# An attention and gated-convolution kernel: batch 0's q and k loaded six tokens per partition, the gates' second half copied out by ScalarE, and a searched order of work

## The chip, the cores and the metric

The kernel runs on 1 core of one Trainium2 chip. The metric is the device time of one execution in microseconds (us), lower is better. A plain run of the kernel before is timed three times; one more execution is taken with the hardware profiler.

## The reference, cut to what matters

Two stages, fused by the kernel: attention with a local window of 96 tokens, 8 global tokens and a linear distance bias, then a projection, a convolution over the whole sequence by FFT, two gates and an output projection.

```python
# q, k, v: (4 batches, 8 heads, 768 tokens, 64);  n_global = 8, n_local = 96
scores = q @ k.transpose(0, 1, 3, 2) / sqrt(64)
rel = pos[:, None] - pos[None, :]
keep = (pos[None, :] < 8) | ((rel >= 0) & (rel < 96))
dist = where(is_global & ~is_local, 96, abs(rel))
a = softmax(where(keep, scores - slopes[h] * dist, -1e9))
x = (a @ v) as (4, 768, 512)
x1, x2, x3 = split(x @ w_proj)              # w_proj: 512 x 1536
conv = irfft(rfft(x2, axis=1) * rfft(filter, axis=0))
out = (x1 * conv * x3) @ w_out              # float32
```

## The kernel before, in words

**Data.** Everything between the loads and the output is float16, sums in PSUM are float32. PSUM is eight banks, held as four tiles of two (`bank0` to `bank3`). A key tile is 120 keys behind the 8 global keys; seven of them cover the 768 tokens, in three groups of two, two and three tiles (`GRP`). A head pair (`hp`, 0 to 3) fills the 128 partitions with two heads of 64.

**Attention of a batch** (`attention`): q and k are transposed on TensorE (`transposes`), the copies out of PSUM fill `QT` and `KT`; `scores` gives one group of a head pair; ScalarE takes the exponential into `E` (864 columns); VectorE multiplies by a mask of decays (`E<-E,mask`), except in batch 0, where TensorE adds the distances first (`near` times `slope`), so that batch 0 needs no mask. `values` multiplies with v, which carries a column of ones; `rc` and `xn` normalise; `transpose_x` and its copy give `xT`. Then `gate` makes, for a quarter of the channels (`j`) and half the tokens (`s`), x1 and x3 in two banks: x1 goes to SBUF (`x`), and VectorE multiplies x3, read from PSUM, by x1 into `g` (line 881). There are 32 such gates in the program, 8 per batch. `butterfly` folds `xT` into what the convolution needs.

**Convolution of a batch** (`conv`): `proj`, its copies `ab`, `fwd` (discrete Fourier matrices), the copies `X`, the products with the filter's spectrum (`p1`, `p2`, `sums`), `inv`, the copies `eo`, the mixing (`mix`), `half` and `y*g` (line 1014), six `out` projections per batch, their copies `ot` and the stores.

**Loads.** A transfer that changes float32 to float16 is issued by GpSimd (POOL), which is how k, v, the weights and the filter come, and q of the later batches. Batch 0's q comes in float32 over the SP queue: six tiles of 128 tokens by 8 heads, 1024 pieces of 256 bytes each, into the six output buffers `ot`, and ScalarE or VectorE casts each into `qn` (`load_q`, line 402 for the issue). Batch 0's k tiles (960 pieces of 256 bytes) alternate with its v tiles on POOL, ahead of the weights.

**What sets the order.** The program is a graph of operations (`Plan.op`), each with a modelled cost on every engine that may run it. `schedule` is a list scheduler: it takes the operation that can start first, with ties inside a small slack broken by a rank (its batch's due time, its place in it, and a bias), and picks the engine that ends it first, by the modelled costs plus `FAVOUR` on VectorE. Banks are chosen in the same pass. The engines then run their lists strictly in that order. Where TensorE's list leaves a gap, `fill` puts in multiplications of a dummy tile (`idle`, line 382), so TensorE stays at work. The times in the planner are its own and set only the order.

Of the kernel before, what the change touches and what calls it, by code (L numbers as in the profile page):

```python
# [59 lines left out]
class Op:  # L60
    __slots__ = ("cost", "fn", "preds", "succs", "wait", "tail", "bias", "acq", "use", "n",
                 "start", "end", "ready", "eng", "bytes", "batch", "table", "name", "order", "first", "landed")


class Plan:
# [55 lines left out]
    def schedule(self):  # L121
        for o in self.ops:
            for x in o.preds:
                x.succs.append(o)
            o.ready = 0.0
# [6 lines left out]
        for o in self.ops:  # L132
            o.first = set()
            for b in o.acq:
                for u in b.users:
                    o.first |= self.outer(u, {o}, o)
            o.first -= o.preds | {o}
            o.wait = len(o.preds) + len(o.first)
        after = {}
        for o in self.ops:  # L140
            for x in o.first:
                after.setdefault(x, []).append(o)
        total = {}
        for o in self.ops:
            o.tail = total.get(o.batch, 0.0)
            total[o.batch] = o.tail + o.cost.get("P", 0.0)
        free = {e: BEGIN for e in "PAVGS"}
# [5 lines left out]
        key = lambda o: o.batch[0] + o.batch[1] * o.tail / (total[o.batch] or 1.0) + o.bias  # L153
        while live:
            best = None
            for o in live:
                at = o.ready
                where = None
                if o.acq:
# [8 lines left out]
                    if at == math.inf:  # L168
                        continue
                e, s = min(((e, max(at, free[e])) for e in o.cost),  # L170
                           key=lambda x: (x[1] + o.cost[x[0]] + self.FAVOUR * (x[0] == "V"), x[0]))
                got = (s, key(o), o, e, where)
# [38 lines left out]
        return self.program(self.fill(out))  # L211

    BUSY = 0.225
    FAVOUR = 0.0
# [78 lines left out]
class Fused:  # L293
    PERIOD = 40.0
    NEAR = 3
    LATER = ()
    WL = [], [], [], [(0, 256), (1024, 256), (256, 256), (1280, 256), (512, 512)]
# [25 lines left out]
    def buffers(self):  # L323
# [34 lines left out]
        self.ot = [t(f"ot{i}", [P, DM], F32) for i in range(6)]  # L358
# [59 lines left out]
    def load_q(self, b, t):  # L418
        src = self.q[b, :, P * t:P * t + P, :].rearrange("h p d -> p h d")
        if b == 0:  # L420
            st = self.ot[t].rearrange("p (h d) -> p h d", h=self.H)
            self.load("S", st, src, [("ot", t)], (1024, 256), f"q{t}")
            self.g.op("AV", {"A": act(512), "V": dve(512, 2)}, lambda e: self.copy(
                e, self.qn[:, t], st), r=[("ot", t)], w=[("qn", t)], name="cast")
        else:
            self.load("G", self.qn[:, t], src, [("qn", t)], (1024, 256), f"q{t}")
# [23 lines left out]
    def setup(self):  # L450
# [21 lines left out]
        for lo, hi in ((0, 2), (2, 7)):  # L472
            g.op("V", dve(512 * (hi - lo), 4), lambda _, lo=lo, hi=hi: v.memset(self.kn[0:NG, lo:hi], 0.0),
                 w=[("kz", t) for t in range(lo, hi)], bias=-4500 if lo == 0 else -3500)
# [73 lines left out]
    def distances(self):  # L548
# [33 lines left out]
        for half in range(2):  # L582
            for k in range(2):
# [5 lines left out]
                g.op("AV", {"A": act(216) + act(264), "V": dve(216, 4) + dve(264, 4)}, spread,  # L589
# [5 lines left out]
        for half in range(2):  # L595
            ps = slice(64 * half, 64 * half + 64)
            for hp in range(4):
                dst = self.slope[ps, hp].rearrange("p k c -> p (k c)")
                dst = dst[:, 0:256].rearrange("p (k c) -> p k c", k=2)
                for k in range(2):  # L600
                    g.op("AV", {"A": act(64), "V": dve(64, 2)}, lambda e, ps=ps, hp=hp, k=k: self.times(
# [4 lines left out]
    def masks(self):  # L606
        g, nc, NL, n = self.g, self.nc, self.NL, 216
        v, dg, far, mask = nc.vector, self.dg, self.far, self.mask
        for hp in range(4):
# [13 lines left out]
            g.op("V", 2 * dve(400, 4) + 2 * dve(216, 4), spread, r=["far"] + [  # L623
# [105 lines left out]
    def scores(self, hp, gi, near=False):  # L729
# [27 lines left out]
        more = ([("near", i, k) for i in range(2) for k in range(2)] + [  # L757
# [17 lines left out]
    def values(self, j, c, slot):  # L775
# [43 lines left out]
        g.op("V", 0.09 + 0.05 * nt, lambda _: nc.vector.reciprocal(rc, view()[:, :, :, D:D + 1]),  # L819
             use=bs, w=[key], name="rc")  # L820
        g.op("AV", {"A": 4 * nt * act(D), "V": dve(4 * nt * D, 1, True)}, scaled, use=bs, r=[key],
# [41 lines left out]
    def gate(self, b, j, s):  # L863
# [4 lines left out]
        for o in (0, 2 * self.DM):  # L868
# [12 lines left out]
        g.op("V", dve(h, 1, True), lambda _: nc.vector.tensor_mul(  # L881
            gt[:, j, h * s:h * s + h], pts[1].f32()[:, 0:h], x1), use=[pts[1]], r=[key],
            w=[("g", b % 2, j, s)], name="g")

    def attention(self, b):
        self.g.batch = (self.PERIOD * (b - 1 + self.SHIFT), self.PERIOD * self.LONG)
        for c in range(3):
            new = ([0, 1, 2], [3, 4], [5])[c]
            for t in new:
                self.transposes("q", t, self.qn[:, t], P * t)  # L890
            for t in self.GRP[c]:
                self.transposes("k", t, self.kn[:, t], P * t)
            for i in range(4):
                self.scores(i, c, c < self.NEAR if b == 0 else (i, c) in self.LATER)
# [87 lines left out]
    def mixed(self, js):  # L982
# [4 lines left out]
        def run(_):  # L987
            v.tensor_sub(t, z, u)
            v.tensor_scalar(u, u, 2.0, None, op0=Alu.mult)
            v.tensor_add(z, z, u)  # L990
            v.tensor_sub(u, t, w)
            v.tensor_add(w, t, w)
        self.g.op("V", 4 * dve(512 * n, 2) + dve(512 * n, 4), run, name="mix", w=[
            ("mixed", jp) for jp in js] + [
            ("eo", jp, jj, par) for jp in js for jj in range(2) for par in range(2)])

    def gated(self, b, jps, half):
# [14 lines left out]
        g.op("V", dve(512 * n, 2) + dve(256 * n, 2), join, r=[("mixed", jp) for jp in jps] + [  # L1012
# [47 lines left out]
    def load_first(self):  # L1060
# [3 lines left out]
        for c in range(3):  # L1064
            for t in ([0, 1, 2], [3, 4], [5])[c]:
                self.load_q(0, t)
            if c == 1:
                self.first_rows(vt)
            runs = [(t, 1) for t in self.GRP[c]]
            for t, n in runs:  # L1070
                self.load_run(("kn",), self.kn, self.k, t, n)
            if c == 0:
                self.distances()
# [110 lines left out]
```

## Time and profile before

| | |
|---|---|
| median of 3 runs | 190.96 us (190.31 to 191.09) |
| the profiled execution's own time | 190.2 us |
| its span | 188.4 us |
| TensorE (PE) busy | 174.0 us, of it 11.4 us dummy multiplications |
| VectorE (DVE) busy | 166.1 us |
| ScalarE (ACT) busy | 144.0 us |
| GpSimd (POOL) busy, mostly issuing transfers | 76.6 us |
| TensorE clock granted | 1.0 throughout |

The span runs from the first to the last record; the run's own time is 1.8 us longer. A line such as `L881 DVE ... x32 | 17.1, 549 | 3.9 <-PE ...` says: line 881, 32 instructions, together 17.1 us busy (overlap taken out), 549 ns mean of one, 3.9 us of idle time on the engine just before them and who ended it. In a timeline, the first number is the start and the second the time until the last of the merged instructions ended. In the table by windows, each engine has its busy time and its count of instructions. The waits of one engine do not add to the span unless the chain that ends last runs through them.

### The profile page before, as it was taken

To read this page: it belongs to the slowest core of one execution; us is meant where nothing else is said; L and a number is where in the kernel's file an instruction comes from. 1 tells how busy PE (TensorE), PEld (TensorE's weight loads), DVE (VectorE), ACT (ScalarE), POOL (GpSimd) and SP (SyncE) were. 2 spreads that over 40 slices of the span, in tenths; PEclk is the share of its full clock that TensorE was granted. 3 is DMA by queue.
4 is the path that set the end of the run, shared out by engine and by line. 5 is a ranking of instruction groups with operands and counts; after the bars stand their busy time and mean duration, and the time that the engine had idled before them with its cause. 6 is when DMAs were issued, how large, how long until landed. Compare 5 with 4: busy or idle time off the path is not lost.

```text
span 188.4 us, 4561 instructions
## 1 busy us (share of the span) xinstructions
PE 174.0 (92%) x1742; PEld 105.7 (56%) x1742; DVE 166.1 (88%) x378; ACT 144.0 (76%) x292; POOL 76.6 (41%) x97
## 2 busy tenths in 40 slices
PE   7877999999899999899898999999998999999891
PEld 2345886656445667575355567754466675447440
DVE  6898875998999969999997869999999999999960
ACT  7389983568999999988967669859869576588352
POOL 8799993599989999993000000000000000000000
PEclk9999999999999999999999999999999999999999
DMA  6999999999999999999053000000260000005244
GB/s 134 197 167 149 153 196 209 154 153 152 143 171 145 154 141 140 142 151 132 4 220 117 0 3 0 3 0 2 80 257 1 5 0 0 3 29 194 111 165 169
DMA packets 90916, 20.47 MB, mean 109 GB/s; under 512 B 83816, under 2 KB 87824, under 8 KB 90896
## 3 DMA queue, kind: packets, MB, share of 16 engines
q0 software_dynamic: 80912, 12.14, 95.6%
q1 hardware_dynamic: 9984, 8.06, 13.6%
q8 instruction: 13, 0.21, 0.5%
q14 instruction: 7, 0.06, 0.1%
HBM read 25.84 MB, written 6.29 MB: 171 GB/s over the span
## 4 chain that ended last, share of the span: by engine, by line
DVE 42%; PE 32%; ACT 13%; issue 4%; SPq 4%; DMA 3%; DVEq 0%; ACTq 0%
PE bank L873 13%; PE bank L970 5%; DVE E L772 4%; SPq L402 4%; DVE g L881 4%; ACT E L765 4%; DMA ot<-in_q_dram 3%; DVE xn L814 3%; DVE y L1014 3%; PE bank L922 2%; PE bank L944 2%; DVE pp L1039 2%; ACT xn L818 2%; ACT QT L386 2%; PE bank L790 2%
## 5 line engine op out<-in xcount | busy, mean ns | idle before, releaser
L873 PE MATMUL bank<-xT,w 128*128 128x384 f16 x256 | 45.0, 326 | 0.2 <-ACT xT L386 0.2
L765 ACT ACTIVATE E<-bank 128x864 f16<-128x864 f32 x48 | 40.1, 910 | 1.2 <-PE bank L751 0.6
L873 PEld LDWEIGHTS <-w 128*128 128x128 f16 x256 | 24.3, 98 | 16.3 <-issue 1.3
L402 POOL DMA_DIRECT2D kn<-in_k_dram x28 | 26.6, 960 | 0.7 <-issue 0.5
L402 POOL DMA_DIRECT2D vn<-in_v_dram x28 | 25.6, 928 | 2.5 <-DMA w<-in_moe_w_proj_dram 1.9
L390 ACT ACTIVATE x<-bank 128x384 f16<-128x384 f32 x29 | 14.7, 508 | 12.7 <-PE bank L873 10.5
L970 PE MATMUL bank<-wo,y 128*128 128x512 f16 x96 | 21.9, 379 | 1.1 <-DVE y L1014 1.0
L772 DVE TENSOR_TENSOR E<-E,mask 128x864 f16<-128x864 f16 x36 | 20.5, 594 | 1.2 <-ACT E L765 1.1
L881 DVE TENSOR_TENSOR g<-bank,x 128x384 f16<-128x384 f32 x32 | 17.1, 549 | 3.9 <-PE bank L873 3.6
L390 ACT ACTIVATE ot<-bank 128x512 f32<-128x512 f32 x21 | 12.5, 597 | 8.2 <-PE bank L970 8.1
L402 POOL DMA_DIRECT2D qn<-in_q_dram x18 | 16.2, 910 | 5.0 <-DMA g<-in_moe_filter_fft_dram 3.5
L751 PE MATMUL bank<-QT,KT 64*128 64x216 f16 (+2 forms) x224 | 15.8, 241 | 2.0 <-ACT E L765 0.9
L970 PEld LDWEIGHTS <-y 128*128 128x128 f16 x96 | 9.0, 98 | 13.1 <-DVE y L1014 3.1
L790 PE MATMUL bank<-vn,E 128*128 128x65 f16 x224 | 15.5, 193 | 0.9 <-ACT E L765 0.8
L814 DVE TENSOR_TENSOR xn<-bank,rc 128x512 f16<-128x512 f32 (+1 forms) x21 | 16.1, 771 | 0.2
L390 ACT ACTIVATE ab<-bank 128x512 f16<-128x512 f32 x21 | 12.5, 611 | 4.0 <-PE bank L922 3.9
L790 PEld LDWEIGHTS <-E 128*128 128x128 f16 x224 | 14.0, 97 | 2.6 <-DVE E L772 0.7
L795 PE MATMUL bank<-vn,E 128*128 128x65 f16 x192 | 15.2, 193 | 0.0
L386 ACT CAST eo<-bank 128x384 f16<-128x384 f32 x29 | 12.9, 509 | 1.7 <-PE bank L947 1.2
L751 PEld LDWEIGHTS <-KT 64*128 64x128 f16 x224 | 8.5, 94 | 9.2 <-issue 5.8
L386 ACT CAST X<-bank 128x512 f16<-128x512 f32 x21 | 11.9, 606 | 2.2 <-PE bank L700 2.1
L795 PEld LDWEIGHTS <-E 128*128 128x128 f16 x192 | 13.2, 97 | 0.6 <-issue 0.3
(141 smaller groups left out, 361.6 us busy)
## 6 DMA issues: line engine op xcount, KB each, us to landing
out_dram<-ot SPq DMA_DIRECT2D x24, 256.0 KB, 2.6
kn<-in_k_dram POOLq DMA_DIRECT2D x28, 120.0 KB, 6.0
vn<-in_v_dram POOLq DMA_DIRECT2D x28, 120.0 KB, 6.7
qn<-in_q_dram POOLq DMA_DIRECT2D x18, 128.0 KB, 6.7
ot<-in_q_dram SPq DMA_DIRECT2D x6, 256.0 KB, 5.8
w<-in_moe_w_proj_dram POOLq DMA_DIRECT2D x4, 256.0 KB, 6.6
g<-in_moe_filter_fft_dram POOLq DMA_DIRECT2D x1, 768.0 KB, 11.9
w<-in_moe_w_proj_dram POOLq DMA_DIRECT2D x1, 512.0 KB, 8.6
```

Of the source, the lines that this page charges most:

```text
L386: {"A": nc.scalar.copy, "V": nc.vector.tensor_copy, "G": nc.gpsimd.tensor_copy}[e](out, in_)
L390: self.nc.scalar.mul(out, in_, c)
L402: return self.g.op(eng, 0.57 + 0.00035 * nbytes[0] if eng == "G" else 0.5, lambda _: e.dma_start(dst, src), w=w, r=r, nbytes=nbytes, name= ...
L751: nc.tensor.matmul(bs[hh].f32()[:, off:off + w], self.KT[hs, hp, P * m:P * m + P], self.QT[hs, hp, KL * m:KL * m + w], start=(off == 0 and ...
L765: g.op("A", act(864), lambda _: nc.scalar.activation(eo, bs[0].two()[:, :, 0:432].rearrange("p h (m w) -> p h m w", m=2), Act.Exp, scale=s ...
L772: g.op("V", dve(864, 2), lambda _: nc.vector.tensor_mul(eo, eo, mk), r=[("E", hp, gi), ("mask", hp)], w=[("E", hp, gi)], name="masked")
L790: nc.tensor.matmul(o[:, n, hh], ef[:, at:at + P], vt[:, t, 2 * hp + hh, :], start=first, stop=(t == 0), skip_group_check=True)
L795: nc.tensor.matmul(o[:, n, hh], ef[:, at:at + P], vt[:, t - 1, 2 * hp + hh, :], start=False, stop=True, skip_group_check=True)
L814: nc.vector.tensor_mul(to, o[:, :, :, 0:D], rc.to_broadcast([P, 2, 2 * nt, D]))
L873: nc.tensor.matmul(bk.f32()[:, 0:h], self.w[:, c, o + P * j:o + P * j + P], self.xT[:, c, h * s:h * s + h], start=(c == 0), stop=(c == 3))
L881: g.op("V", dve(h, 1, True), lambda _: nc.vector.tensor_mul(gt[:, j, h * s:h * s + h], pts[1].f32()[:, 0:h], x1), use=[pts[1]], r=[key], w ...
L970: nc.tensor.matmul(bk.f32(), y[:, c, P * t:P * t + P], self.wo[:, c, :], start=(c == 0), stop=(c == 3))
```

## The change

Four things change.

1. **q and k of batch 0** come by head pair: `load_pair` loads two heads with six consecutive tokens in each partition, so 256 pieces of 1536 bytes, all eight transfers on the SP queue (q into the `ot` buffers, k into `h1` and `h2`). The cast writes them as `[token of six][head]`. `transpose_pair` transposes six times 128 columns into one bank, and the copy out of PSUM puts the tokens back in order: it reads with a step of 128 columns where the old copy read neighbours. k is unpacked in two copies, and the global columns are spread per head pair. `attention(0)` now takes all three score groups of a head pair before the next pair. POOL keeps only v, weights and filter for batch 0.
2. **The gates** (`TWICE` holds all 32): ScalarE copies x3 out of PSUM as float16, and VectorE multiplies two float16 tiles in SBUF.
3. **The planner's numbers**: modelled costs of some operations (`near`, `spread`, `rc`, `xn` on ScalarE, `vfirst`), `FAVOUR` 0.1 instead of 0, `mixed` as five operations instead of one, the slopes on ScalarE only.
4. **The order**: before laying the list, `schedule` adds to ranks and engine preferences what a list of 40 seeds draws (`shake`), found by a search.

The diff, cut to its core:

```diff
+    def schedule(self):
+        self.prepare()
+        for seed in self.SEEDS:
+            self.shake(seed)
+        return self.program(self.fill(self.lay()))
+
+    def shake(self, seed):
+        r = random.Random(seed)
+        if r.random() < 0.4:
+            groups = sorted({(o.name, o.batch) for o in self.ops if o.eng not in "GS"})
+            g, by = r.choice(groups), r.gauss(0.0, 5.0)
+            lean = r.gauss(0.0, 0.3)
...
-        key = lambda o: o.batch[0] + o.batch[1] * o.tail / (total[o.batch] or 1.0) + o.bias
+            o.rank = o.batch[0] + o.batch[1] * o.tail / (total[o.batch] or 1.0) + o.bias + o.noise
...
-    FAVOUR = 0.0
+    SEEDS = (5, 6, 10, 30, 55, 82, 86, 89, 90, 94, 176, 184, 198, 209, 262, 321, 423, 503, 556,
...
+    FAVOUR = 0.1
...
+    TWICE = frozenset((b, j, s) for b in range(4) for j in range(4) for s in range(2))
...
+    def load_pair(self, what, hp):
+        hs, n = slice(2 * hp, 2 * hp + 2), what + "n"
+        if what == "q":
+            st, keys = self.oq[:, 768 * hp:768 * hp + 768], [("ot", i) for i in range(6)]
+        else:
+            st = (self.h1, self.h2)[hp // 2].bitcast(F32).rearrange("p a b -> p (a b)")
+            st, keys = st[:, 768 * (hp % 2):768 * (hp % 2) + 768], []
+        self.load("S", st.rearrange("p (h x) -> p h x", h=2),
+                  (self.q if what == "q" else self.k)[0, hs].rearrange("h (p r) d -> p h (r d)", r=6),
+                  [("stage", what, hp)], (256, 1536), what)
+        to = (self.qn if what == "q" else self.kn)[:, 0:6, hs].rearrange("p r h d -> p h r d")
+        self.g.op("AV", {"A": act(768), "V": 0.9}, lambda e: self.copy(
+            e, to, st.rearrange("p (h r d) -> p h r d", h=2, r=6)), r=[("stage", what, hp)] + keys,
+            w=[(n, "pair", hp)], name="cast")
+
+    def transpose_pair(self, what, hp):
...
+            for r in range(6):
+                nc.tensor.transpose(b.f16()[:, P * r:P * r + P], src[:, r, 2 * hp:2 * hp + 2, :],
+                                    self.ident)
...
+            g.op("AV", {"A": act(768), "V": dve(768, 1, True)}, lambda e: self.copy(
+                e, self.QT[:, hp].rearrange("p (n r) -> p n r", r=6),
+                b.f16()[:, 0:768].rearrange("p (r n) -> p n r", r=6)), use=[b],
+                w=[("QTp", hp)], name="qT")
...
-        g.op("V", dve(h, 1, True), lambda _: nc.vector.tensor_mul(
-            gt[:, j, h * s:h * s + h], pts[1].f32()[:, 0:h], x1), use=[pts[1]], r=[key],
-            w=[("g", b % 2, j, s)], name="g")
+        x3, ko = gt[:, j, h * s:h * s + h], ("g", b % 2, j, s)
+        if (b, j, s) in self.TWICE:
+            g.op("A", act(h), lambda _: nc.scalar.copy(x3, pts[1].f32()[:, 0:h]), use=[pts[1]],
+                 w=[ko], name="x3")
+            g.op("V", dve(h, 2), lambda _: nc.vector.tensor_mul(x3, x3, x1), r=[key], w=[ko], name="g")
+            return
...
     def attention(self, b):
         self.g.batch = (self.PERIOD * (b - 1 + self.SHIFT), self.PERIOD * self.LONG)
+        if b == 0:
+            for hp in range(4):
+                self.transpose_pair("q", hp)
+                self.transpose_pair("k", hp)
+                for c in range(3):
+                    self.scores(hp, c, True, True)
...
-        for c in range(3):
-            for t in ([0, 1, 2], [3, 4], [5])[c]:
-                self.load_q(0, t)
-            if c == 1:
+        for hp in range(4):
+            self.load_pair("q", hp)
+            self.load_pair("k", hp)
+            if hp == 0:
+                self.distances()
+            if hp == 1:
                 self.first_rows(vt)
...
+        for t in range(7):
+            self.load_run(("vn", 0), vt, self.v, t, 1)
```

**Where instructions move.** First, GpSimd's list at the start of the program, before (`dg` and `far` are the tables of distances from which the score biases are made):

```order
masks.py:199 AFFINE_SELECT ident<-ident 128x128
L402 DMA kn<-in_k_dram 120x8x64 x2
L557 IOTA dg 128x216
L562 AFFINE_SELECT dg<-dg 128x216 x2
L557 IOTA dg 128x48
...
L402 DMA vn_63<-in_v_dram 120x8x64 x2
L577 AFFINE_SELECT far<-far 8x120 x2
L402 DMA kn<-in_k_dram 120x8x64 x2
L402 DMA vn_63<-in_v_dram 120x8x64 x2
L402 DMA kn<-in_k_dram 120x8x64 x3
L402 DMA vn_63<-in_v_dram 120x8x64 x3
L402 DMA w<-in_moe_w_proj_dram 128x4x256 x3
```

and the same place now:

```order
masks.py:199 AFFINE_SELECT ident<-ident 128x128
L631 IOTA dg 128x216
L636 AFFINE_SELECT dg<-dg 128x216 x2
...
L440 DMA vn_63<-in_v_dram 120x8x64
L651 AFFINE_SELECT far<-far 8x120 x2
L440 DMA vn_63<-in_v_dram 120x8x64 x6
L440 DMA w<-in_moe_w_proj_dram 128x4x256 x4
```

Seven k transfers left this queue, two of which stood ahead of the tables of distances, and the weights follow v at once.

Second, ScalarE's list from the first bias table to the fourth exponential, before (buffer `bank_121` to `bank_124` are the PSUM tiles, `E_67` to `E_70` the four head pairs' exponentials, `mask` the decays for the later batches):

```order
L386 COPY near<-dg 64x264
L612 ACTIVATE mask<-dg 128x216
...
L386 CAST qn<-ot_103 128x512
L386 COPY QT<-bank_122 128x4x128
L386 CAST qn<-ot_104 128x512
L765 ACTIVATE E_67<-bank_123 128x2x2x216
L765 ACTIVATE E_68<-bank_124 128x2x2x216
L765 ACTIVATE E_69<-bank_121 128x2x2x216
```

and now (`h_85` and `h_86` hold k of pairs 0, 1 and 2, 3 in float32):

```order
L424 COPY near<-dg 64x264
L424 CAST qn<-ot 128x2x6x64
L686 ACTIVATE mask<-dg 128x216
L424 CAST kn<-h_85 128x2x6x64
L424 COPY KT<-bank_116 128x6x120
L424 COPY KT<-bank_116 128x120
L424 CAST qn<-ot 128x2x6x64
L424 CAST kn<-h_86 128x2x6x64
...
L840 ACTIVATE E_67<-bank_118 128x2x2x216
L840 ACTIVATE E_67<-bank_119 128x2x2x216
L424 CAST kn<-h_86 128x2x6x64
L840 ACTIVATE E_67<-bank_116 128x2x2x216
```

The exponentials go by head pair, and the cast of the last pair's k stands between the second and the third of them.

Third, VectorE's list where the first gates are multiplied, before (`x_95` to `x_98` are the four x1 buffers, `g_87` the gates of batch 0):

```order
L814 TENSOR_TENSOR xn_72<-bank_124,rc_106 128x2x384
L881 TENSOR_TENSOR g_87<-bank_123,x_95 128x384
L881 TENSOR_TENSOR g_87<-bank_121,x_96 128x384
L881 TENSOR_TENSOR g_87<-bank_122,x_97 128x384
L881 TENSOR_TENSOR g_87<-bank_124,x_98 128x384
L386 COPY xT<-bank_124 128x2x288
```

and now:

```order
L571 TENSOR_SCALAR y<-y 128x512
L960 TENSOR_TENSOR g_87<-g_87,x_95 128x384
L931 TENSOR_TENSOR xo<-xab,xcf 128x2x256
L960 TENSOR_TENSOR g_87<-g_87,x_96 128x384
L933 TENSOR_SCALAR xcf<-xcf 128x2x256
```

The gates no longer read a bank, and they alternate with the folds of the butterfly, where before four of them stood in a row.

138 lines of the change are left out of this document (83 added, 55 removed).

## The prediction

> **What bounds the kernel now.** I read the page first: busy times, slices, and the chain that ended last by engine.
>
> ```profile
> span 188.4 us, 4561 instructions
> PE 174.0 (92%) x1742; PEld 105.7 (56%) x1742; DVE 166.1 (88%) x378; ACT 144.0 (76%) x292; POOL 76.6 (41%) x97
> DVE  6898875998999969999997869999999999999960
> ACT  7389983568999999988967669859869576588352
> DVE 42%; PE 32%; ACT 13%; issue 4%; SPq 4%; DMA 3%; DVEq 0%; ACTq 0%
> ```
>
> No engine rules alone: VectorE holds most of the chain and is full from the middle on, TensorE is nearly as full, ScalarE is full only from slice 10 to 17. So I cut the span at three places of the program: the first gate (27.0 us), the product `y*g` of batch 0 (93.8, both kernels stand there at the same TensorE work, dummies left out), and the last `y*g` (182.2). The products end here, in VectorE's timeline:
>
> ```profile
> 91.95 1.82 DVE L1014 TENSOR_TENSOR y<-y,g 128x1536 f16<-128x1536 f16 x2
> ...
> 181.65 0.56 DVE L1014 TENSOR_TENSOR y<-y,g 128x768 f16<-128x768 f16 x1
> ```
>
> From the table by windows, first all work, then that of line 382 (the dummies) alone:
>
> ```profile
> 0.00:27.00 27.00, 22.83 (x325) 15.20 (x326) 22.20 (x78) 20.96 (x53) 25.05 (x40) 1.00 1.68 164
> 27.00:93.80 66.80, 63.65 (x636) 38.68 (x633) 60.66 (x131) 57.23 (x111) 51.56 (x58) 1.00 2.16 144
> 93.80:182.20 88.40, 85.20 (x778) 50.88 (x776) 83.22 (x170) 64.00 (x128) 0.00 (x0) 1.00 0.15 58
> 42.00:84.00 42.00, 39.49 (x434) 24.71 (x433) 38.96 (x87) 40.27 (x81) 39.57 (x45) 1.00 2.46 149
> 24.00:42.00 18.00, 18.00 (x221) 12.30 (x216) 14.35 (x36) 10.79 (x19) 12.48 (x15) 1.00 1.84 179
> ...
> 27.00:93.80 66.80, 2.06 (x8) 0.66 (x8) 1.00 2.16 144
> 93.80:182.20 88.40, 1.41 (x5) 0.49 (x5) 1.00 0.15 58
> ```
>
> The columns are PE, PEld, DVE, ACT, POOL. In the last stretch VectorE works 83.2 of 88.4 us and ScalarE 64.0: there VectorE sets the pace. In 42 to 84 ScalarE works 40.3 of 42 and VectorE 39.0: both are full. TensorE can give back its idle time and its dummies: 66.8 - 63.65 + 2.06 = 5.2 us in the middle, 88.4 - 85.2 + 1.41 = 4.6 after it.
>
> **The change part by part.** The groups of instructions with shapes, of which I use busy time over count:
>
> ```profile
> L881 DVE TENSOR_TENSOR g<-bank,x 128x384 f16<-128x384 f32 x32 | 17.1, 549 | 3.9 <-PE bank L873 3.6 <-ACT x L390 0.2
> L1046 DVE TENSOR_TENSOR X<-pp 128x512 f16<-128x512 f16 x8 | 3.3, 414 | 0.0
> L1010 DVE TENSOR_TENSOR y<-eo 128x256 f16<-128x256 f16 x4 | 1.1, 282 | 0.0
> L386 ACT CAST eo<-bank 128x384 f16<-128x384 f32 x29 | 12.9, 509 | 1.7 <-PE bank L947 1.2
> L818 ACT ACTIVATE xn<-bank,rc 128x64 f16<-128x64 f32 x28 | 6.0, 371 | 1.1 <-DVE rc L819 1.1
> L814 DVE TENSOR_TENSOR xn<-bank,rc 128x512 f16<-128x512 f32 x14 | 9.5, 682 | 0.1
> L814 DVE TENSOR_TENSOR xn<-bank,rc 128x768 f16<-128x768 f32 x7 | 6.6, 949 | 0.1
> L386 DVE COPY xT<-bank 128x480 f16<-128x480 f16 x11 | 4.3, 394 | 2.7 <-PE bank L835 2.7
> L386 ACT COPY xT<-bank 128x480 f16<-128x480 f16 x5 | 2.9, 588 | 0.5 <-PE bank L835 0.5
> L386 DVE COPY QT<-bank 128x512 f16<-128x512 f16 x5 | 2.1, 412 | 0.1
> L392 DVE TENSOR_SCALAR ot<-bank 128x512 f32<-128x512 f32 x3 | 2.0, 669 | 0.0
> L390 ACT ACTIVATE ot<-bank 128x512 f32<-128x512 f32 x21 | 12.5, 597 | 8.2 <-PE bank L970 8.1
> ```
>
> *Gates.* The product costs VectorE 17.1/32 = 0.53 us. From SBUF in float16 it lies between the 256- and 512-column products of two float16 tiles, 0.28 and 0.41: 0.345, so 0.19 less, 32 times 6.1 us. ScalarE gains a copy of 384 columns out of PSUM, like `eo`: 12.9/29 = 0.445, 32 times 14.2.
>
> *Moves between engines*, counted in the two orders: all 28 `xn` pieces leave ScalarE (-6.0) for three on VectorE (2 x 0.68 + 0.95 = +2.3); six `xT` copies go the other way (-2.3, +3.5); two `ot`, an `ab` and an `x` too (-2.6, +2.3). With the start's changes, VectorE comes out about 7 us lighter and ScalarE 17 heavier: the two together do more work than before, and what counts is where each of them was waited for. `mixed` as five operations issues the same five instructions, so it costs nothing by itself; other operations of VectorE may now stand between them, which only the order decides.
>
> *The start*, for which I read ScalarE's timeline, TensorE's, and the chain:
>
> ```profile
> 2.59 1.82 ACT L390 ACTIVATE slope<-ident 64x64 bf16<-64x64 f16 x11 [0.36 <-DVE slope L594]
> 7.85 1.39 ACT L386 COPY near<-dg 64x216 bf16<-64x216 bf16 x4 [3.43 <-DVE dg L571]
> 9.26 1.32 ACT L612 ACTIVATE mask<-dg 128x216 f16<-128x216 bf16 x6
> 12.19 0.62 ACT L386 CAST qn<-ot 128x512 f16<-128x512 f32 x1
> 24.44 3.24 ACT L765 ACTIVATE E<-bank 128x864 f16<-128x864 f32 x4
> ...
> 12.42 0.54 PE L742 MATMUL bank<-near,slope 64*128 64x432 bf16 x4
> 27.02 5.36 PE L873 MATMUL bank<-xT,w 128*128 128x384 f16 x32
> 32.22 0.50 PE L835 MATMUL bank<-ident,xn 128*128 128x128 f16 x6
> ...
> 33.98 0.26 PE L521 MATMUL bank<-cst,one 1*128 1x256 f16 x1
> ...
> 8.27 5.85 DMA ot<-in_q_dram
> 100.05 3.40 ACT xn L818 x16
> ```
>
> ScalarE's 3.4 us wait for `dg` goes, since two k transfers leave POOL ahead of the tables. Its new list up to the twelfth exponential: 16 slopes at 0.165 = 2.65, six `near` at 0.35 = 2.1, five casts at 0.8 (0.62 for 512 columns, and 0.69 ns for each more, as between `eo` and `ot`) = 4.0, two unpackings of k at about 1.05 (a cast's time and a small piece) = 2.1, ten masks at 0.2 = 2.0, twelve exponentials at 3.24/4 = 0.81 = 9.7: 22.6 us from 2.4, so 25.0 without a wait, against 27.7 (24.44 + 3.24). With a microsecond of waits for first scores, and then values, `xn`, `trx` and `xT` of the last pair (0.5 + 0.9 + 0.4 + 0.5), the first gate starts near 28.0. By then all of batch 0's scores and values and the angles of the Fourier tables are done, which before came after the first gates, from 32.22 to 34.24, 2.0 us; six transposes of 0.06 are still to come, so 1.7. A gate at 28.0 now stands for one at 28.7: the start gives -0.7 (-2.5 if nothing waits, +1.5 if ScalarE stands another two microseconds).
>
> On TensorE, 21 dummies and then 24 transposes and eight dummies stand ahead of the first scores. At the rates of the trace (0.21 to 0.42 a dummy, 0.06 a transpose) they end near 11, so scores that began at 12.42 may begin a microsecond sooner, no more. The memsets of k's global rows shrink to one; VectorE has time for that either way. POOL is rid of seven transfers, so v, the weights and the filter come sooner; no row of before shows a matmul waiting for the weights, so that is worth nothing here.
>
> The unpacking of q on VectorE (four times 768 columns, step 128) is in no row. Its ends are 1.5 x 0.42 = 0.62, if the step costs nothing, and the 768-column float32 row, 0.95; I take 0.9, nearest to the second, where no two 16-bit values lie side by side either. By the Trainium skill's "VectorE: DVE Perf Modes", section "Mode 2×_1P — pack two bf16 into one 32-bit read", two per cycle need 16-bit neighbours at step 1, so the step speaks against the change: the four would cost 3.8 instead of 2.5. Either way ScalarE's list is longer here, and the sum stays.
>
> *Middle, 27 to 93.8.* By counts, ScalarE gets 3.7 more from the twelfth exponential to the first `ot`, VectorE 4.2 less from the first gate to `y*g`. ScalarE idles 66.8 - 57.2 = 9.6 here, 7.2 of it in 24 to 42 (18 - 10.8), just where batch 0's gates stand: the 16 copies fit there in part (7.1). After 42 there is little room, so of TensorE's 5.2 I take 2.0 (0 to 5.2).
>
> *After 93.8.* By counts, VectorE has 5.5 less: 16 products (3.0), five copies of `xT` (2.0), two of `ot` (1.3), four other copies (2.2), against two `xn`, two masked tiles and an `eo` more (3.0). Neighbours overlap a little in the rows (they add up to 185 where the page has 166.1), so 5.0 of it is time. ScalarE has 11.5 more, and 24.4 idle. The 3.4 us of ScalarE's 16 `xn` pieces, in the chain at 100, become two VectorE products, 1.4. TensorE caps the gain at 4.6; I take its idle time, 3.2 (0 to 4.6). What is late next is TensorE itself. The tail behind the last `y*g` (6.2) holds the same twelve projections and stores: 0.
>
> The sum: -0.7 - 2.0 - 3.2 = -5.9 on a span of 188.4, so 182.5; with the 1.8 around it 184.3, against 190.2 for the profiled execution. The runs' median of 190.96 is 0.8 above that: **185.0**.
>
> **The rivals.**
>
> *ScalarE becomes the bound (188.0).* For it: 40.3 of 42 us in 42 to 84. If the copies of x3 don't find the early gap, the 3.7 stay in the middle; its 2.0 are lost, and a microsecond more. Against: the twelve exponentials of batch 0 are over earlier. By the Trainium skill's "ScalarE: Activation LUTs", section "Rules for kernel authors", simple multiplications and additions belong on VectorE, not ScalarE; by that the gate edit is a loss, 14.2 added for 6.1 saved. Where VectorE sets the pace, the saved part alone counts, and that is most of the span.
>
> *Slower: the last k holds up ScalarE (195).* ScalarE's list is in order, and the cast of pair 3's k stands ahead of ten exponentials, at 2.4 + 2.65 + 2.1 + 3.2 + 1.05 + 0.6 + 1.6 = 13.6 us. Its transfer is the ninth on SP, behind 2.8 MB. In the chain the sixth q tile, after 1.6 MB, landed at 8.27 + 5.85 = 14.1: 0.13 MB/us from about 2 us. At that rate k lands at 26, ScalarE stands for 12 us, and gains of 5.9 are outweighed from a landing after 19.5. Against it is what the stores show, in pieces of 2 KB:
>
> ```profile
> 96.00:96.50 0.50, 0.50 (x4) 0.26 (x3) 0.50 (x2) 0.36 (x1) 0.00 (x0) 1.00 1.04 401
> ```
>
> At 401 GB/s, 3.2 MB take 8 us, so 10.5; beside v, perhaps 13.
>
> *The order doesn't hold (190.3).* It was laid with modelled costs, and an operation that comes late holds up all behind it. If the stalls only move, just the start's 0.7 remains. For it: the order before was laid in the same way, and still TensorE idles for 3.2 us in each of the two long stretches.
>
> *The product stays slow (189.5).* If two float16 tiles from SBUF still took 0.53, the 6.1 would be lost. The rows at 512 and 256 columns speak against it.
>
> **How the numbers follow.** The forecast has 0.70, ScalarE as the bound 0.12, the order that doesn't hold 0.08, the late k 0.06, the slow product 0.04. The terms' good ends give -2.5 - 5.2 - 4.6 = -12.3, 178.7; their bad ends +1.5. From 179.5 to 190.6 the range takes in the forecast nearly whole and most of the cases of little change. About 0.5% (1 us) is what a measurement can tell from no change. Faster by more: 0.70 + 0.09 + 0.02 + 0.02 = 0.83; within: 0.09; slower: 0.08.
>
> **What would show it.** Right: the twelfth exponential ends by 26.5, the first gate starts by 28.5; `y*g` of batch 0 comes near 91; the products take 0.35 us and VectorE's busy time falls to about 159, ScalarE's rises to about 160; the stretch to the last `y*g` shrinks to 85. Wrong: ScalarE waits for a transfer ahead of k's last cast; ScalarE at 97% or more from 30 to 90 with `y*g` not earlier; or TensorE's idle time, dummies included, no smaller after 94.

## The result, and the profile after

The changed kernel takes 183.62 us (median of four runs, 182.05 to 183.98) against 190.70 for the kernel before on the same chip: a ratio of 0.961 (95% interval 0.955 to 0.967). Here and below a ratio leaves out executions more than 1.5% above their kernel's fastest and the medians keep them, so the two can differ. The forecast was 185.0, range 179.5 to 190.6. The total fits; the way there does not, and neither does the cause that I gave it.

The page of the changed kernel, the same rows as those shown of before:

```profile
span 182.2 us, 4507 instructions
PE 170.5 (94%) x1734; PEld 105.2 (58%) x1734; DVE 156.5 (86%) x368; ACT 156.2 (86%) x312; POOL 71.6 (39%) x90
PE   7999399999999798999999999999999999999990
PEclk9999969999999999999999999999999999999999
PE 64%; ACT 12%; DVE 9%; DMA 6%; POOL 5%; issue 2%; DVEq 0%; POOLq 0%; ACTq 0%
```

VectorE held 42% of the chain before and holds 9% now; TensorE holds 64% and is full but for one hole, slice 4 (counted from 0), behind which its granted clock drops. The same three marks as in the prediction, from the timelines of TensorE (first gate) and VectorE (`y*g`):

```profile
32.59 4.71 PE L948 MATMUL bank<-xT,w 128*128 128x384 f16 x28
...
89.71 1.82 DVE L1101 TENSOR_TENSOR y<-y,g 128x1536 f16<-128x1536 f16 x2
...
174.15 1.02 DVE L1101 TENSOR_TENSOR y<-y,g 128x768 f16<-128x768 f16 x2
```

The table by windows cut there (PE, PEld, DVE, ACT, POOL), then the first three windows for the dummies of line 420 alone:

```profile
0.00:32.60 32.60, 27.74 (x365) 18.12 (x366) 23.12 (x72) 26.64 (x66) 22.47 (x36) 0.95 1.77 205
32.60:91.53 58.93, 56.99 (x561) 34.55 (x561) 56.64 (x134) 54.43 (x103) 46.45 (x51) 1.00 2.28 131
91.53:175.18 83.65, 83.00 (x799) 51.45 (x796) 76.71 (x164) 72.79 (x143) 2.69 (x3) 1.00 0.23 63
175.18:182.20 7.02, 2.76 (x12) 1.09 (x12) 0.00 (x0) 2.34 (x4) 0.00 (x0) 1.00 0.54 210
...
0.00:32.60 32.60, 9.89 (x32) 0.95 1.77 205
32.60:91.53 58.93, 0.00 (x0) 1.00 2.28 131
91.53:175.18 83.65, 0.59 (x2) 1.00 0.23 63
```

The first gate comes 5.6 us later than before (32.6 against 27.0). The middle is 7.9 shorter (58.9 against 66.8), the long last stretch 4.8 (83.65 against 88.4), the tail 0.8 longer: -6.2 of span. In the middle and the last long stretch TensorE is idle or on dummies for 1.94 and 1.24 us, where it was 5.2 and 4.6.

The start lost time, and ScalarE's and TensorE's timelines name the wait:

```profile
14.27 0.83 ACT L424 CAST kn<-h 128x768 f16<-128x768 f32 x1 [0.89 <-DMA h<-in_k_dram]
15.01 3.22 ACT L840 ACTIVATE E<-bank 128x864 f16<-128x864 f32 x4
...
24.00 0.89 ACT L840 ACTIVATE E<-bank 128x864 f16<-128x864 f32 x1 [3.61 <-PE bank L825]
25.46 4.02 ACT L840 ACTIVATE E<-bank 128x864 f16<-128x864 f32 x5 [0.57 <-PE bank L825]
...
20.51 0.20 PE L865 MATMUL bank<-vn,E 128*128 128x65 f16 x1 [2.21 <-DMA vn<-in_v_dram]
21.71 0.19 PE L865 MATMUL bank<-vn,E 128*128 128x65 f16 x1 [0.61 <-DMA vn<-in_v_dram]
```

ScalarE waits 3.61 us for scores, but TensorE stands in front of those scores in values that wait for the last tiles of batch 0's v. Yet these tiles come no later than before. The last three of v, issues and time to landing, first before, with the first matmul that needs one of them, then now:

```profile
L402 POOL DMA_DIRECT2D vn<-in_v_dram x3: 903/903/903, 15.6 to 17.4; - x3
DMA to landing us min/median/max: 6.1/6.1/6.2
...
26.29 0.19 PE L790 MATMUL bank<-vn,E 128*128 128x65 f16 x1
```

```profile
L440 POOL DMA_DIRECT2D vn<-in_v_dram x3: 901/901/1106, 8.9 to 10.9; - x3
DMA to landing us min/median/max: 10.8/10.8/11.6
```

The last tile landed at 17.4 + 6.2 = 23.6 us before and lands at 10.9 + 10.8 = 21.7 now. But the old order asks for these three at 26.3, when all had landed; the new one, pair by pair, has the values of all tiles ahead of the scores of two head pairs, and stands for v from 18.3 on. So v is late for the new order, not later than it was.

A tile of v does take longer to land, 10.8 us for 6.1. What moved in the first 12 us, of this kernel and then of before (queue q1 is SP's, q0 POOL's):

```profile
q1 hardware_dynamic: 2201, 3.11, 79.8%
q0 software_dynamic: 757, 0.09, 11.5%
```

```profile
q0 software_dynamic: 4234, 0.50, 66.4%
q1 hardware_dynamic: 5918, 1.49, 64.7%
```

The columns are pieces (packets), MB and their time as a share of 16 engines' span; a piece of POOL's counts here with some 120 bytes, as it arrives in float16. SP's q and k, now in pieces of 1536 bytes, took nearly all of it, and v, which POOL had been issuing since 3.35 us, got 0.09 MB; in the next 2 us, with SP's pieces through, it moved 2224 pieces. No run changes SP's load alone, so what part of v's 21.7 us it causes is not shown.

### The profile page after: what moved, and what is told of

Its sections match the earlier page's. It is cut to its first block, busy times and chain, and to the rows that moved or that the text cites. A ratio compares the mean times of both kernels' runs of the same rounds, so it can differ in the third digit from the quotient of the medians.

```text
span 182.2 us, 4507 instructions
## 1 busy us (share of the span) xinstructions
PE 170.5 (94%) x1734; PEld 105.2 (58%) x1734; DVE 156.5 (86%) x368; ACT 156.2 (86%) x312; POOL 71.6 (39%) x90
## 4 chain that ended last, share of the span: by engine, by line
PE 64%; ACT 12%; DVE 9%; DMA 6%; POOL 5%; issue 2%; DVEq 0%; POOLq 0%; ACTq 0%
PE bank L948 17%; PE bank L1009 11%; PE bank L1057 10%; DMA vn<-in_v_dram 6%; PE bank L774 5%; PE bank L1031 5%; PE bank L788 4%; PE bank L825 4%; POOL vn L440 4%; ACT E L840 3%; PE bank L910 3%; PE bank L865 3%; PE bank L870 2%; ACT KT L424 2%; ACT xT L424 1%
## 5 line engine op out<-in xcount | busy, mean ns | idle before, releaser
L948 PE MATMUL bank<-xT,w 128*128 128x384 f16 x256 | 43.7, 326 | 0.1
L440 POOL DMA_DIRECT2D vn<-in_v_dram x28 | 27.0, 971 | 6.2 <-PE bank L788 3.3
L440 POOL DMA_DIRECT2D kn<-in_k_dram x21 | 19.3, 925 | 18.0 <-PE bank L910 15.9
L428 ACT ACTIVATE ot<-bank 128x512 f32<-128x512 f32 x23 | 14.1, 614 | 5.9 <-PE bank L1057 5.7
L889 DVE TENSOR_TENSOR xn<-bank,rc 128x512 f16<-128x512 f32 (+1 forms) x24 | 18.5, 775 | 0.4
L865 PE MATMUL bank<-vn,E 128*128 128x65 f16 x224 | 15.9, 193 | 3.0 <-DMA vn<-in_v_dram 2.8
L958 ACT CAST g<-bank 128x384 f16<-128x384 f32 x32 | 15.8, 508 | 2.0 <-PE bank L948 1.6
L870 PE MATMUL bank<-vn,E 128*128 128x65 f16 x192 | 15.7, 193 | 0.0
L428 ACT ACTIVATE ab<-bank 128x512 f16<-128x512 f32 x22 | 13.6, 635 | 1.5 <-PE bank L1009 1.5
L424 ACT CAST X<-bank 128x512 f16<-128x512 f32 x22 | 12.8, 621 | 0.6 <-PE bank L774 0.6
L774 PE MATMUL bank<-ab,fwd 128*128 128x512 f16 x40 | 11.6, 379 | 1.4 <-DVE xT L424 1.4
```

What stands on the lines that cost most here:

```text
L428: self.nc.scalar.mul(out, in_, c)
L440: return self.g.op(eng, 0.57 + 0.00035 * nbytes[0] if eng == "G" else 0.5, lambda _: e.dma_start(dst, src), w=w, r=r, nbytes=nbytes, name= ...
L774: self.nc.tensor.matmul(b.f32(), self.fwd[:, f], src(i, t), start=(n == 0), stop=(n == len(terms) - 1))
L865: nc.tensor.matmul(o[:, n, hh], ef[:, at:at + P], vt[:, t, 2 * hp + hh, :], start=first, stop=(t == 0), skip_group_check=True)
L870: nc.tensor.matmul(o[:, n, hh], ef[:, at:at + P], vt[:, t - 1, 2 * hp + hh, :], start=False, stop=True, skip_group_check=True)
L889: nc.vector.tensor_mul(to, o[:, :, :, 0:D], rc.to_broadcast([P, 2, 2 * nt, D]))
```

## The experiments

The kernels of each batch ran on one chip beside the kernel before, whose medians were 190.63 to 190.92; the ratio is to that.

### Which part pays

Theory A, that of the prediction: the lighter VectorE pays, through the gate edit, and the order only carries it. Theory B: the searched order pays.

**Gate edit alone** (kernel before, nothing else changed):

```diff
-        tensor_mul(gt[...], pts[1].f32()[:, 0:h], x1)      # VectorE, out of PSUM
+        nc.scalar.copy(x3, pts[1].f32()[:, 0:h])           # ScalarE
+        nc.vector.tensor_mul(x3, x3, x1)                   # VectorE, two f16 tiles
```

> The kernel before with the gate edit alone: x3 copied out by ScalarE, the product of two float16 tiles on VectorE; loads, planner numbers and search as before. Theory A (the relief of VectorE pays, 6 us of busy time, where VectorE set the pace): 185 to 187.5, the last stretch (batch 0's y*g to the last y*g) down from 88.4 to about 84.5. Theory B (the searched order pays, and the gate edit only fills ScalarE): 189 to 192, the last stretch no shorter than 87.

191.56 us, ratio 1.006 (1.002 to 1.010), its last stretch 87.2 us, as theory B had it. **The changed kernel without the search** (`SEEDS = ()`):

> The changed kernel without the 40 seeds: same operations, same modelled costs, the order as the list scheduler lays it by itself. Theory A: most of the gain stays, 184 to 186. Theory B: most of it goes, 188 to 191. The start is the same in both, with the first gate near 32 us, since TensorE's first list hardly changes.

191.47 us, ratio 1.001 (0.996 to 1.005). The first gate, expected near 32 us by both, came at 35.05: TensorE's first list did change. **Without the search and without the gate edit** (also `TWICE = frozenset()`), so new loads, unpacking and costs alone:

> The changed kernel without the seeds and with the gates as before (x3 read from PSUM by VectorE): what is left is batch 0's loading by pairs and the planner's numbers. Theory A: slower than the run without seeds by 3 to 5 us, 188 to 191 or above the kernel before, since the start ends 5 us later than before's (first gate 32 for 27, with 1.7 us more done). Theory B: within 1.5 us of the run without seeds.

190.91 us, ratio 0.999 (0.995 to 1.003). Theory A fell with these three. The groups of the product show that the relief itself was there, first of the gate edit alone, then of the change without the search, then of the change (busy and mean, then the idle time ahead of it):

```profile
L884 DVE TENSOR_TENSOR g<-g,x 128x384 f16<-128x384 f16 x32 | 10.7, 351 | 4.7 <-ACT g L882 4.7
```

```profile
L958 DVE TENSOR_TENSOR g<-g,x 128x384 f16<-128x384 f16 x32 | 10.9, 354 | 2.9 <-ACT g L956 2.8
```

```profile
L960 DVE TENSOR_TENSOR g<-g,x 128x384 f16<-128x384 f16 x32 | 10.8, 352 | 0.8 <-ACT g L958 0.7
```

Busy and idle, the row of the product cost VectorE 17.1 + 3.9 = 21.0 us before, 15.4 with the gate edit alone, 13.8 without the search, 11.6 with the change. So this row took 5.6 us less of VectorE in a kernel that was 0.6% slower. Of the 6.4 us less that the product was busy (17.1 to 10.7), 0.8 went into longer waits ahead of it, now for the copy, which stands right ahead of the product in an order that no search had laid:

```profile
29.68 0.36 DVE L884 TENSOR_TENSOR g<-g,x 128x384 f16<-128x384 f16 x1 [0.52 <-ACT g L882]
30.98 0.36 DVE L884 TENSOR_TENSOR g<-g,x 128x384 f16<-128x384 f16 x1 [0.94 <-ACT g L882]
32.27 0.36 DVE L884 TENSOR_TENSOR g<-g,x 128x384 f16<-128x384 f16 x1 [0.94 <-ACT g L882]
```

More of it went into other work: its page has VectorE busy for 163.3 us, only 2.8 less than before, with 386 instructions for 378, and ScalarE for 152.8, 8.8 more instead of the 15.5 of its copies. That fits a planner that finds ScalarE taken and gives more to VectorE.

That the order pays could still mean that it pays by itself. So I ran the search anew, on the planned time, for programs that lack one part. **A searched order alone** (kernel before, with `noise`, `lean` and 30 seeds of its own) and **a searched order on the new loads, product out of PSUM** (19 seeds, `TWICE` empty):

> The kernel before with one thing more: the noise and lean of the planner, and a list of seeds of its own that a search over this kernel's planned times accepted; loads, unpacking, costs and the product out of PSUM are those of before. Theory O (the searched order pays by itself, whatever the loads and the product are): 185 to 188 us, since the kernel changed without seeds lost all 7 us and the order is what was lost. Theory J (the order pays only on top of the gate edit, which takes 6.7 us off VectorE that a better order can then use): 189 to 192 us. Marks: under O the stretch from the end of batch 0's gating product to the last one is 84 to 86 us against 88.4 before; under J 87 to 89.

> The changed kernel with the product out of PSUM as before (TWICE empty) and a list of seeds of its own, searched for that program. Theory O: 184.5 to 188 us, the start 3 to 5 us later than before and the rest of the order giving 6 to 8 back. Theory J: 189 to 191.5, as the two kernels without seeds (190.9 and 191.5), VectorE busy near 165 us and over 93% in the stretch after batch 0's gating product.

190.63 and 189.59 us, ratios 0.994 (0.990 to 0.998) and 0.994 (0.991 to 0.997): both in J's ranges. Theory O fell as A had. (The mark of the stretch after `y*g` was badly chosen: 83.70 and 83.17 us, about as O had it, but a searched order also moves work ahead of that mark.) Of the executions in the first ratio, three with a granted clock of 1.0 took 188.12 to 188.91 us, three at 0.976 to 0.985 took 189.76 to 190.85: still above O's 188, but those at 1.0 are about 1.1% under 190.63, so 0.6% is no cap for what an order wins by itself. What these orders didn't reach shows among ScalarE's waits, in before, then with the searched order on the new loads, then with gate edit alone, then in the change:

```profile
ACT x L390 <- PE bank L873: 10.5, 16, 0.8
```

```profile
ACT x L426 <- PE bank L946: 11.0, 15, 1.5
```

```profile
ACT x L390 <- PE bank L873: 3.3, 16, 0.6
```

```profile
ACT x L428 <- PE bank L948: 2.1, 8, 0.6
```

Ahead of the evacuation of `x` ScalarE waits 10.5 us for the gates' matmuls, 11.0 with a searched order; the gate edit puts its copies in there. My reading is that there is then spare time on VectorE for an order to fill, and not before. The rows agree with it, but no run tests it; nor do they show that no longer search would find a way without the edit.

What remains is J, and its test is **gate edit and searched order on the old loads**, twice, with lists from two searches (45 and 40 seeds):

> The kernel before with the gate edit (ScalarE copies g out of PSUM, VectorE multiplies two f16 tiles) and an order searched for it; loads, unpacking and costs of before. So far the gate edit alone gave a ratio of 1.006 to before, a searched order alone 0.994, loads and costs alone 0.999, loads with the gate edit 1.001, loads with a searched order 0.994, and all three 0.961. Theory J (the searched order pays with the gate edit, whatever the loads): 182 to 186 us, first gate near 28, last stretch 83 to 84.5. Theory T (all three are needed, the gain comes from the loads that let the order begin otherwise): 188 to 190.5. In between, 186 to 188, neither is told.

> As gate_search (the kernel before with the gate edit and a searched order, its own loads), with a second list of seeds from another search. Theory J (gate edit and searched order make the gain together, the loads add nothing that is larger than the difference between two searched orders): 183.5 to 187.5 us, a ratio of 0.962 to 0.982, as two lists on the changed kernel's loads gave 0.961 and 0.976. Theory T (the loads are needed too, and gate_search was the lucky one of its kind): 188 to 191, a ratio above 0.985. VectorE's wait for ScalarE's copy ahead of the gate products is 0.7 to 1.5 us in all under J, against 4.7 with the gate edit and no search.

186.85 and 185.00 us, ratios 0.975 (0.968 to 0.982) and 0.968 (0.963 to 0.974). The first alone decided nothing (the range between), the second falls in J's. The mark of the last stretch (83 to 84.5) failed again, with 88.0 and 90.3 us: the gain of the second lies ahead of it, where `y*g` of batch 0 ends at 86.4 us for 93.8 before. In the second the wait for the copy is nearly as short as in the change, and the first gate stands where the old loads let it:

```profile
L919 DVE TENSOR_TENSOR g<-g,x 128x384 f16<-128x384 f16 x32 | 10.8, 347 | 1.1 <-ACT g L917 1.0
...
28.40 2.77 PE L908 MATMUL bank<-xT,w 128*128 128x384 f16 x16
```

VectorE is busy for 164.5 us there, against 166.1 before: what the gate edit frees is filled again, and the 3.2% don't need a lighter VectorE.

**Another list on the changed kernel** (29 other seeds) asks whether the change's own 40 are special:

> The changed kernel with another list of 29 seeds, which a new search over the planned times accepted; all else is the same. If any order pays that such a search finds for this program: 182.5 to 186 us, first gate between 31 and 33, stretch after batch 0's gating product 83 to 85. If the 40 seeds of the change fit the chip in a way that the planned time doesn't show (the loads land otherwise than the plan has it): 187.5 to 190.5 us, most of it lost ahead of batch 0's gating product.

186.28 us, ratio 0.976 (0.971 to 0.981): by its time the first case, a little outside its range (186), but its stretch after the gating product is 81.2, shorter than any, and the loss lies ahead of it. All together, as ratios:

| | order as planned | searched order |
|---|---|---|
| loads and product of before | 1 | 0.994 |
| gate edit | 1.006 | 0.975, 0.968 |
| new loads and costs | 0.999 | 0.994 |
| both | 1.001 | 0.961 (the change), 0.976 |

By these ratios neither gate edit nor order is worth over 0.6% without the other (the intervals reach 1.0%); together they are worth 2.4 to 3.9%. Two lists for one program differ by 0.7 and 1.5%, so what the new loads add is not larger than that spread, and is not told from it.

### What the late v costs

**The planner told** when v's tiles land (13 to 21.7 us; the first four landed 0.6 to 1.7 us later than it was told, at 14.7 to 17.7), with the seeds of the change:

```diff
                 ready = o.landed = dma[e] + 0.5
+                if o.name in self.LANDS:
+                    ready = o.landed = self.LANDS[o.name]
```

> The changed kernel with the planner told when batch 0's v tiles landed in the profile (13, 14.5, 16, 17, 20.5, 20.9, 21.7 us); no data, buffer or wait is changed, only the order that is laid: the scores of pairs 2 and 3 stand ahead of most values. Start theory (TensorE stood for v in its own order, and ScalarE and the clock with it): ScalarE's 3.6 us wait in the start goes, the clock stays at 1.0, the first gate starts at 28.5 to 30 for 32.2, and the time is 180.5 to 182.5. Rival (what comes after makes up for a late start, or the seeds fit only the old times): first gate earlier, but the time 183 to 186.

191.58 us, ratio 0.996 (0.991 to 1.001): the gain is gone, outside both ranges, and in the profiled execution, its slowest, the first gate came at 35.87, later instead of earlier. The seeds are noise on ranks, and with other landing times the same noise is another order, one that no search chose. **The same with seeds searched on that plan** (36 of them):

> The changed kernel with the planner told when the tiles of batch 0's v landed in the profile (13 to 21.7 us), and seeds searched on that plan. With the old seeds that gave 191.6. If an order that knows the landing puts other work into the pause: TensorE's wait for v of 2.2 us goes, the half clock behind it too, 180.5 to 183 us, below the changed kernel. Rival: the first gate still needs all of v and stays at 31.5 to 33, and the time is as with the change, 183 to 186. Third: orders found on the plan don't hold on the chip, 187 to 191.

184.65 us, ratio 0.964 (0.958 to 0.970): the search alone turns 0.996 into 0.964. It is the second case: the first gate is at 31.91, and the time no better than the change's. TensorE still stands for 3.31 us ahead of values at 23.5, and the half clock still follows. Planning around v doesn't bring v.

**v as a quarter:** two of eight heads are loaded and the others are zeros, in the order of the change; the output is not the reference's.

```diff
-        rows = src[0, :, ...]
-        self.load("G", dst[NG:P, t:t + n, :, 0:self.D], rows, ...
+        rows = src[0, 0:2, ...]
+        self.load("G", dst[NG:P, t:t + n, 0:2, 0:self.D], rows, ...
```

> The changed kernel with only two of the eight heads of batch 0's v loaded and zeros in the other six (a VectorE memset of about 3 us at the start), in the same order of work: the output is not the reference's. It takes the wait for v away. Start theory (all of the first gate's delay behind v reaches the end): last tile of v by 15 us, first gate at 27.5 to 29 instead of 32.2, time 179.0 to 180.5. Rival (the middle stretch is bound by something else, the tables or the other loads, and gives back less): first gate as early, but time 181.5 to 183.5. Third: v was not what held the first gate, which stays at 31 to 32, and the time is as the changed kernel's, 183 to 184.5.

181.55 us, ratio 0.952 (0.949 to 0.956), just inside the rival's range. TensorE no longer waits for v. From its timelines (ScalarE, TensorE, VectorE):

```profile
9.95 0.83 ACT L424 CAST qn<-ot 128x768 f16<-128x768 f32 x1
21.88 4.85 ACT L840 ACTIVATE E<-bank 128x864 f16<-128x864 f32 x6
...
29.84 4.71 PE L948 MATMUL bank<-xT,w 128*128 128x384 f16 x28
...
171.76 1.03 DVE L1101 TENSOR_TENSOR y<-y,g 128x768 f16<-128x768 f16 x2
```

The first gate comes 2.75 us sooner than with the change (there 32.59, not the 32.2 of the expectations), the last `y*g` 2.4: what the start gives reaches the end. The gate is still later than both theories had it (27.5 to 29), as my memset took a part back: ScalarE's first cast starts at 9.95 here, at 7.28 with the change, and from there ScalarE sets the pace. By the medians this kernel gains 2.1 us, which I take for an estimate of what standing for v costs, and not for a bound: of the change's four executions, the one with a granted clock of 1.0 took 182.05 us, 0.5 above this kernel, and the three at 0.99 took 183.4 to 184.0.

**Dummies in the pause:** behind the wait TensorE's clock is low in the change (table by windows; the seventh number is the clock):

```profile
20.00:22.00 2.00, 0.75 (x14) 0.56 (x15) 0.00 (x0) 0.39 (x2) 1.24 (x2) 1.00 1.51 189
22.00:23.00 1.00, 1.00 (x20) 0.48 (x16) 0.64 (x3) 0.00 (x0) 1.00 (x3) 0.67 1.45 197
23.00:25.00 2.00, 1.70 (x16) 1.07 (x16) 1.94 (x8) 0.89 (x1) 2.00 (x3) 0.50 1.39 201
25.00:26.00 1.00, 1.00 (x22) 0.96 (x19) 1.00 (x7) 0.54 (x1) 1.00 (x2) 0.63 1.27 208
```

If the clock is either full or half, the last three rows make 0.66 + 2.0 + 0.74 = 3.4 us at half. Sixteen dummies ahead of the late values:

```diff
+            if slot == 0 and j == 0 and c == 2 and not self.warmed:
+                self.warmed = True
+                self.busy(16, bs[0])
```

> The changed kernel with 16 dummy matmuls more on TensorE ahead of the first values that wait for the last tiles of v; everything else stands in the same order. Clock theory (the half clock at 22.5 to 26 us is what follows the pause, and costs): granted clock 1.0 in 22 to 26 us, the near scores 0.54 instead of 0.90 us, first gate at 30.7 to 31.3 instead of 32.2, time 182.3 to 183.0. Rival (the exponentials pace that stretch, or the gap is refilled behind it): first gate at 32.2 and 183.4 to 184.2. If the dummies end after v lands, up to 0.5 us is lost again.

183.83 us, ratio 0.963 (0.959 to 0.968), no different from the change: the rival's time, at neither theory's first gate. The clock stayed at 1.0 and the near scores at 0.54 us, but the first gate came at 33.29. Two rows say why that settles nothing: pair 3's k was waited for longer in this execution, and the dummies ran until 23.96, past v's last tile (23.0).

```profile
16.34 0.83 ACT L424 CAST kn<-h 128x768 f16<-128x768 f32 x1 [1.50 <-DMA h<-in_k_dram]
...
20.35 3.61 PE L420 MATMUL bank<-idle 128*128 128x512 f16 x16
```

What the low clock costs by itself stays open: the change's execution at 1.0 was 1.4 to 1.9 us faster than its others, but nothing tells what else differed in it.

## Why the prediction was right, and where it was not

*The start, forecast -0.7: measured about +4.* The gate comes 5.6 us later. Without dummies TensorE had 14.9 us of work ahead of it before (22.8 less 7.9 of dummies) and has 27.74 - 9.89 = 17.9 now. About 1.4 of the 2.9 more is the same work at the half clock: the near rows took 0.90, 0.90 and 0.82 us there instead of 0.54, the scores 0.54 and 0.59 instead of 0.36. So 1.5 came forward, where I counted 1.7, and the start lost 5.6 - 1.5 = 4.1. The step that failed is the 28.0 for the first gate, "with a microsecond of waits for first scores": I walked ScalarE's list alone, and its waits come to 0.89 + 3.61 + 0.57 = 5.07 us, 4.18 of them for scores that TensorE holds back while it stands for v. "POOL is rid of seven transfers, so v, the weights and the filter come sooner" is true of v's last three tiles, and of no help: I didn't ask when the new order needs them. I asked that of k, which waits 0.9 us. (My terms also add up to 28.3 and not to 28.0.) ScalarE's list itself was right: the twelfth exponential ends at 25.46 + 4.02 = 29.5, and without its waits (0.89, 3.61, 0.57) at 24.4, where I had 25.0. In the kernel with a quarter of v it ends at 26.7, 2.7 of that the late first cast: 24.0.

*The middle, forecast -2.0 (0 to -5.2): measured -7.9, less the 1.5 that came forward, -6.4.* TensorE gave 3.3 us of idle time and dummies (5.2 to 1.9). The other 3.1 lie in its busy time, so past my cap: the mark doesn't stand at the same TensorE work, 893 matmuls are ahead of it for 922, and four of those 29 are transposes that no longer exist. By luck the errors of start and middle cancel: `y*g` of batch 0 ends at 91.5, forecast near 91.

*After 93.8, forecast -3.2 (0 to -4.6): measured -4.8.* TensorE gave 3.4 us of idle time and dummies. The rest lies past my cap, in its busy time (83.79 to 82.41 us without dummies, with some 23 matmuls more), which I had taken as fixed. Over the span it fell from 162.6 to 160.0, the 1.4 of the half clock included, with the same matmuls but four transposes: the 256 of the gates take 45.0 us in before and 43.7 now at the same mean of 326 ns, so in another order they overlap more. *The tail, forecast 0: measured +0.8*; twelve matmuls lie behind the mark, ten before.

*The attribution was wrong.* VectorE came out 9.6 us lighter (166.1 to 156.5), where I had about 7; the product's 0.345 us held (10.8/32 = 0.338 by the same reckoning), and ScalarE's rise came out at 12 where I had 17, though its copy takes more (15.8/32 = 0.49, not 0.445). But I booked the gain to these, and the order as the risk. Gate edit alone is slower by 0.6%; the seeds, which I gave no term, are a condition for it: without them the ratio is 1.001. The question that I missed stands in the diff: the product now waits for one copy more, on another engine, and what does VectorE do meanwhile?

*The unpacking of QT*, taken as 0.9, bounds 0.62 to 0.95:

```profile
L424 DVE COPY QT<-bank 128x768 f16<-128x768 f16 x4 | 3.7, 948 | 1.2 <-PE bank L482 1.1
```

It took 0.948, the upper end, 3.8 for the four, as the rule of the Trainium skill's "VectorE: DVE Perf Modes", section "Mode 2×_1P — pack two bf16 into one 32-bit read", had it.

*The rivals.* ScalarE as the bound: in 42 to 84 us it works 39.5 and VectorE 39.7, so neither alone. The rule of the Trainium skill's "ScalarE: Activation LUTs", section "Rules for kernel authors", that simple arithmetic belongs on VectorE, speaks against the edit as I read it; that agrees with the order as planned (1.006) and not with a searched one (0.994 to 0.975 and 0.968). The late k came with 0.9 us, not 12; with it my first sign of being wrong, a wait of ScalarE ahead of k's last cast, did appear. The order held here; that one need not was shown by the old seeds on a new plan.

## What to carry to other kernels

Here work taken off a full engine was worth nothing until the order put something in its place: when an edit splits one step over two engines, look for the wait in the row of the second half, and re-plan before judging the edit. A list of seeds fits one plan only: with seven other landing times in the planner it had to be searched again. And when an edit reorders the consumers of a load that it doesn't touch, ask of that load when it lands and when the new order first needs it; walk the list of every engine, not only of the one that looks full.

## What the runs showed of the hardware

SP's pieces of 1536 bytes moved 3.11 MB in the first 12 us while POOL's of 256 (float32, some 120 as written) got 0.09 MB; with 256 bytes on both, 1.49 and 0.50 had moved. By the Trainium skill's "DMA: Bandwidth & Descriptors", section "Queues, rings and completion order", an engine takes a whole packet of descriptors from each queue in turn, which would favour large pieces in bytes; here SP led in number too, 2201 pieces to 757, and no run shows why.

After TensorE had worked 0.31 us in 18 to 20 us and 0.75 in 20 to 22, with no single wait above 2.21 us, its clock was at half for 3.4 us, and the near scores took 0.90 us instead of 0.54; with 16 dummies in the pause it stayed at 1.0.
